# Another place and another bank for the transposed maxima of the second attention block

## The chip, the cores and the metric

The kernel runs on one core of a Trainium2 chip. The metric is the device time of one execution in microseconds. The engines that matter here: TensorE (PE in the profile; PEld is its loading of weights), VectorE (DVE), ScalarE (ACT), GpSimd (POOL), and SyncE (SP), which issues the DMAs. TensorE writes to PSUM, which has eight banks of 512 float32 values for each of 128 partitions.

## The reference

Two attention blocks with the same shapes and separate inputs, their outputs side by side. Block A attends only to the last 256 positions, block B to all.

```python
S, D, H = 2048, 512, 32          # Dh = 16
qkv = (x @ wqkv) -> q, k, v      # per head, [S, 16]
scores = q @ k.T * Dh ** -0.5    # [S, S] per head
# A only: positions outside 0 <= i - j < 256 get -1e9
p = softmax(scores, axis=-1)
out = concat_heads(p @ v) @ wo
# result: concatenate([out_A, out_B], axis=-1)
```

## The kernel before

Work is cut into *units*: one block, one group `g` of four heads (`HG`), one chunk `c` of 512 queries. Block B has 8 groups by 4 chunks, so 32 units; a unit runs over 16 key tiles of 128 keys. One key tile of one unit is a *step*.

A softmax needs each query's maximum before its exponentials. So the scores are computed twice. The first time, queries lie on the partitions: `max2` (L358) multiplies, and VectorE reduces 512 keys of each head to a maximum (L373). After the last of a unit's pieces, `max_finish` (L432) reduces what is left on VectorE (L441) and lets GpSimd negate it and split it into three bfloat16 parts (L450 to L457), in the tile `nm`. `max_rows` (L460) transposes `nm` on TensorE (L465), ScalarE copies the result from PSUM (L467, tile `ntr`), and two DMAs (L472) write it as additional rows into the query operand `oq`. The second time, keys lie on the partitions: `scores` (L488) multiplies the keys with those extended queries (L498), so that the maximum is already taken off, and ScalarE exponentiates (L505). `weigh2` (L520) multiplies the exponentials with the values (L529).

The end of the kernel's code emits block B in a fixed order, a string that is run through again and again, two steps for each pass:

```python
ORDER = "ssm4mssMs2msms2sM"
LAST = "ssss4"
```

`s` is one head's scores of the step `k`. `m` is one head's piece of maxima, `M` two heads'. A digit is that many quarters of a step's values (`weigh2`), two steps behind the scores. So a pass has 8 `s`, 8 heads' maxima (4 `m`, 2 `M`) and 8 quarters. The maxima are those of the unit after the one whose scores run, four pieces ahead of it. When none is left, `LAST` takes the place of `ORDER`.

Each kind of result has PSUM banks of its own (`view`, L194): three for the scores ("e", five in `LAST`, where the maxima's pair is added), two behind one another for `M` ("p"), one for the weighted values ("o"), and two that `room()` (L702) hands out in turn in this part of the kernel ("s"): to each `m`, to the output projection, and to the transposed maxima. A bank of "e" is taken with `M.take("e")`, which picks the one that a small time model holds free first, and given back with `release`.

A unit's last maxima are emitted at the end of a pass, where the loop's `k` is 12 of the unit's 16 steps. `max_finish` follows at once, and the unit is put on the list `rows` with a step from which it may be transposed. Ahead of the first `s` of a step the loop also emits planned work (`todo`): loads of keys, queries and values, the normalisation of finished units. The waiting unit of `rows` is looked up at the same place.

All engines run their instructions in the order of emission, each waiting for what it needs.

Of the kernel before, what the change touches and what calls it, by code (L numbers as in the profile page):

```python
# [118 lines left out]
def attention_kernel(ctx: ExitStack, tc: tile.TileContext, xT, wqk, wv, wo, out):  # L119
# [9 lines left out]
    M = Model()  # L129
# [64 lines left out]
    def view(bank):  # L194
        pool, n = bank
        first, width = {"e": (0, 1), "o": (3, 1), "p": (4, 2), "s": (6, 1)}[pool]
        n = first + width * n + (pool == "e" and n > 2)
        return ps_all[:, n] if width == 1 else ps_all[:, n:n + 2]
# [159 lines left out]
    def max2(g, c, qt, kc, heads, ps):  # L358

        m = maxima(1, g, c).rearrange("p (a r) q k -> p a r q k", a=2)  # L360
        early = g == 0 and c == 0 and heads[0] < 2
        if not early:
            follow(("k", 1, g))
            follow(("q", 1, g, c))
        for n, j in enumerate(heads):
            r, a = divmod(j, 2)
            rows = slice(ROW[a], ROW[a] + KS)
            q, k = (qe[0], ke()) if early else (opq[1, g, c][:, r], opk2(g)[:, r])
            nc.tensor.matmul(ps[:, n], q[rows, 128 * qt:128 * qt + 128], k[rows, kc * QC:kc * QC + QC], start=True,  # L369
                             stop=True)  # L370
            t = M.pe("h", 118, 0 if early else loaded(1, g, c))
        r, a = divmod(heads[0], 2)
        nc.vector.tensor_reduce(out=m[:, a:a + len(heads), r, qt, kc], in_=ps, axis=AX.X, op=ALU.max)  # L373
        return M.run("DVE", 65 + 533 * len(heads), t)
# [85 lines left out]
    def max_rows(b, g, c):  # L460
        n = f"{b}_{g}_{c}"
        nm = parts["nm"]
        bank, ps = room()
        ps = ps.bitcast(BF16)
        nc.tensor.transpose(ps[:48, :128], nm.rearrange("p a s j q -> p (a s j q)"), ident)  # L465
        nt = sb.tile([48, 128], F32, name=f"ntr_{n}", tag="ntr")
        nc.scalar.activation(nt, ps[:48, :128], AF.Copy)  # L467
        t = M.run("ACT", 200, M.pe("f", 60, ready["nm", b, g, c]))
        release(bank, t)
        for a in range(2):  # L470
            ready["q", b, g, c] = M.dma(12, t)
            nc.sync.dma_start(opq[b, g, c][ROW[a] + KS:ROW[a] + KM].bitcast(F32).rearrange(  # L472
                "s r (q t) -> s (r q) t", t=128), nt[24 * a:24 * a + 24])
# [14 lines left out]
    def scores(b, g, c, kt, j, heads=1, pieces=((),)):  # L488

        n = f"{b}_{g}_{c}_{kt}"  # L490
        pr, a0 = divmod(j, 2)
        banks = [M.take("e") for _ in range(heads)]
        ps = [view(bank) for bank in banks]
        w = QC if b else sum(x[3] for x in pieces)
        for k, col, q0, n1 in [(kt, 0, 0, QC)] if b else pieces:
            for x in range(heads):
                rows = slice(ROW[a0 + x], ROW[a0 + x] + KM)
                nc.tensor.matmul(ps[x][:, col:col + n1], opk2(g)[rows, pr, 128 * k:128 * k + 128],  # L498
                                 opq[b, g, c][rows, pr, q0:q0 + n1], start=True, stop=True)
            t = M.pe("h", 235 if b else 12 + n1 / 2.4, ready["q", b, g, c])  # L500
        if a0 == 0:
            pts[b, g, c, kt, pr] = sb.tile([128, 2, QC], F32, name=f"p_{n}_{pr}", tag="p", bufs=2 * AHEAD)
        p = pts[b, g, c, kt, pr]
        for x in range(heads):
            nc.scalar.activation(p[:, a0 + x, :w], ps[x][:, :w], AF.Exp, scale=SCALE)  # L505
            done = M.run("ACT", 60 + w / 1.2, t)
            M.release(banks[x], done)
        if b == 0:

            for d, sign, base in ((0, 1, 0), (2, -1, -1)):  # L510
                cols = [col // 128 + x for k, col, q0, n1 in pieces for x in range(n1 // 128)
                        if 4 * c + q0 // 128 + x - k == d]
                for x in cols:
                    v = p[:, :, 128 * x:128 * x + 128]
                    nc.gpsimd.affine_select(out=v, in_=v, pattern=[[0, 2], [sign, 128]], compare_op=ALU.is_ge,  # L515
                                            fill=zero_fill, base=base, channel_multiplier=-sign)
                    done = M.run("Pool", 360, done)
        ready["p", b, g, c, kt] = done
# [161 lines left out]
    def settle():  # L680

        while soon and soon[0][0] <= M.t["PE"]:
            heapq.heappop(soon)[2]()
# [9 lines left out]
    slot = [False, 0]  # L693

    def bank():
        return M.bank(pool())

    def pool():

        return min(("e",) if ns else ("e", "p"), key=lambda x: max(M.t["PE"], M.bank(x)))  # L700

    def room():  # L702

        if slot[0]:
            slot[1] ^= 1
            return None, view(("s", slot[1]))
        while bank() >= M.NEVER:
            advance()
        b = M.take(pool())
        return b, view(b)[:, 0] if b[0] == "p" else view(b)  # L710

    def release(b, t):
        if b is not None:
            M.release(b, t)

    def pop():
        now[0], _, f, a = heapq.heappop(todo)
        f(*a)
        made.add((f, *a))
# [6 lines left out]
    def advance():  # L726
        if gen[0] is None:
            while operands(proj[0][3]) >= M.NEVER:
                if soon:
                    heapq.heappop(soon)[2]()  # L730
                else:
                    pop()
            M.t["PE"] = max(M.t["PE"], operands(proj[0][3]))
            begin(heapq.heappop(proj)[3])
        try:
            next(gen[0])
        except StopIteration:
            gen[0] = None
            made.add(gen[1])
# [145 lines left out]
    while todo_a or gen[0]:  # L885
# [45 lines left out]
        if x == "t":  # L931
            un = nts.pop(0)
            max_rows(*un)
            made.add((max_rows, *un))
        elif x == "s":
            un, (m, pieces), a, z = flat[i]
# [63 lines left out]
    ns, nq, nm, half, got = 0, -8, AHEADM, 0, 0  # L1000
    t0 = M.t["PE"]
    rows = []
    while nq < 4 * len(steps):
        if nm == len(mx) and len(M.banks["e"]) == 3:
            M.banks["e"] += [M.t["PE"]] * 2
        for x in ORDER if nm < len(mx) else LAST:
            k = ns // HG
            if x == "s" and k < len(steps):
                if ns % HG == 0:
                    t = k * STEP  # L1010
                    M.t["PE"] = max(M.t["PE"], t0 + int(1000 * k * STEP))
                    settle()
                    while todo and todo[0][0] <= t:
                        pop()
                    if rows and rows[0][0] <= k:
                        max_rows(*rows.pop(0)[1])
                scores(1, *steps[k], ns % HG)
                ns += 1
            elif x in "Mm" and nm < len(mx):
                u, g, c, qt, kc = mx[nm]  # L1020
                if x == "M":
                    h = (0, 1)
                    two = view(("p", 0))
                else:
                    h = (2 + half,)
                    half ^= 1
                    two = room()[1][:, None]
                max2(g, c, qt, kc, h, two)
                got += len(h)
                if got == HG:  # L1030
                    nm += 1
                    got = 0
                    if nm % 16 == 0:
                        max_finish(1, g, c)
                        rows.append((k + 2, (1, g, c)))
            elif x.isdigit():
                if 0 <= nq < 4 * len(steps):
                    g, c, kt = steps[nq // 4]
                    q = nq % 4
                    weigh2(g, c, kt, 128 * q, 128 * (q + int(x)))  # L1040
                    if kt == NT - 1 and q + int(x) == 4:
                        unit_end(1, g, c)
                nq += int(x)
                if int(x) == 4:

                    t = k * STEP
                    two = heapq.nsmallest(2, proj)
                    if two and two[-1][0] <= t and max(operands(y[3]) for y in two) <= M.t["PE"]:
                        now[0] = t
                        for _ in two:  # L1050
                            advance()
                            while gen[0]:
                                advance()
                            t0 += 2400
# [29 lines left out]
```

## Time and profile before

| | us |
|---|---|
| median of 3 runs | 1860.56 |
| lowest, highest | 1859.86, 1864.45 |
| the profiled execution | 1862.03 |
| span of its instructions | 1860.3 |

| engine | busy us | share of the span |
|---|---|---|
| PE | 1837.5 | 99% |
| DVE | 1544.4 | 83% |
| ACT | 1408.5 | 76% |
| POOL | 469.8 | 25% |

The shares are means over the whole kernel, which has stages with different limits: block A and the projections up to about 540 us, block B's loop from there to about 1775 us, and then the last scores, values and output projections. Busy PE means that a matmul is in flight, not that the next could not have come earlier.

In the rows of the profile, `L373 DVE` is an instruction of line 373 on VectorE; `out<-in` are the program's tiles; `xN` is a count. In a group's row the figures behind the bar are the busy time in us and the mean duration in ns, then the engine's idle time just before these instructions and what ended most of it. In a row of waits: who waited, for whom, us in total, times, longest. In a row of the timeline: start and length in us, and in brackets the idle time ahead of it and what ended it; neighbours of one kind are merged into one row. In a row by stretches: the stretch and its length, then busy time (and instructions) of PE, PEld, DVE, ACT and POOL, the clock granted to TensorE (1.00 is full speed), the DMA engines' share and GB/s.

### The profile page before, as it was taken

How to read it: one execution, taken by the hardware profiler on the slowest of the kernel's cores; microseconds unless marked ns; L12 is line 12 of the kernel's file. 1: busy time of each engine (PE TensorE's matmuls, PEld its weight loads, DVE VectorE, ACT ScalarE, POOL GpSimd, SP SyncE). 2: the span in 40 equal slices, each digit the busy share in tenths (PEclk: the TensorE clock that was granted, in tenths of full speed). 3: DMA queues.
4: the chain of work that ended last, by engine and by line, in shares of the span. 5: the costliest groups of instructions: out<-in, count | busy, mean ns of one | idle time of the engine just before them, and what ended most of it. 6: DMA issues, size and time to landing. Idle time of an engine off the chain costs nothing.

```text
span 1860.3 us, 37278 instructions
## 1 busy us (share of the span) xinstructions
PE 1837.5 (99%) x14376; PEld 923.6 (50%) x14376; DVE 1544.4 (83%) x2320; ACT 1408.5 (76%) x2754; POOL 469.8 (25%) x896
## 2 busy tenths in 40 slices
PE   8999999999999999999999999999999999999999
PEld 6666656666654545444444444444444444444436
DVE  4677686766779777799999999999999999999901
ACT  4456566655558776788888888888888888889873
POOL 0367877654654331000010001000000001010010
PEclk9999999999999999999999999999999999999999
DMA  8755657544563221311300211130031130010002
GB/s 260 208 182 183 210 189 216 149 156 140 170 195 98 80 84 56 84 34 35 75 17 30 57 45 28 28 76 16 16 74 34 28 67 31 17 53 8 30 30 96
DMA packets 129153, 166.68 MB, mean 90 GB/s; under 512 B 23012, under 2 KB 58852, under 8 KB 128964
## 3 DMA queue, kind: packets, MB, share of 16 engines
q1 hardware_dynamic: 128976, 164.31, 30.4%
q8 instruction: 113, 1.85, 0.4%
q14 instruction: 64, 0.52, 0.1%
HBM read 94.49 MB, written 68.19 MB: 87 GB/s over the span
## 4 chain that ended last, share of the span: by engine, by line
PE 94%; DVE 3%; ACT 1%; POOL 1%; DMA 1%; SPq 0%; issue 0%; ACTq 0%; POOLq 0%
PE ps_all L529 29%; PE ps_all L183 19%; PE ps_all L369 19%; PE ps_all L498 19%; PE ps_all L544 4%; PE ps_all L417 3%; DVE mt L373 2%; ACT p L505 1%; PE ps_all L465 1%; DVE mt L427 1%; DMA in<-xT_A 0%; DVE ps_all L426 0%; POOL p L515 0%; POOL x L138 0%; DMA opk<-parts 0%
## 5 line engine op out<-in xcount | busy, mean ns | idle before, releaser
L505 ACT ACTIVATE p<-ps_all 128x512 f32<-128x512 f32 x2432 | 1261.6, 599 | 176.1 <-PE ps_all L498 120.0
L373 DVE TENSOR_REDUCE mt<-ps_all 128x2 f32<-128x1024 f32 x1516 | 1202.3, 868 | 83.7 <-PE ps_all L498 48.4
L498 PE MATMUL ps_all<-oq,opk 51*128 51x512 f32 (+2 forms) x2752 | 781.5, 410 | 7.7 <-ACT p L505 5.8
L369 PE MATMUL ps_all<-opk,oq 48*128 48x512 f32 x2016 | 677.6, 439 | 2.0 <-DVE mt L373 1.9
L529 PE MATMUL ps_all<-p,vt 128*32 128x256 f32 (+1 forms) x6056 | 600.1, 468 | 0.5 <-ACT ou L555 0.5
L498 PEld LDWEIGHTS ps_all<-oq,opk 51*128 51x128 f32 x2752 | 397.1, 185 | 206.6 <-ACT p L505 184.0
L369 PEld LDWEIGHTS ps_all<-opk,oq 48*128 48x128 f32 x2016 | 312.9, 185 | 321.0 <-DVE mt L373 147.9
L450 POOL TENSOR_SCALAR mm<-mm 128x16 f32<-128x16 f32 x31 | 7.9, 254 | 984.2 <-PE ps_all L498 812.8
L529 PEld LDWEIGHTS ps_all<-p,vt 128*32 128x32 f32 x6056 | 119.7, 108 | 220.7 <-issue 210.2
L515 POOL TENSOR_SCALAR_AFFINE_SELECT p<-p 128x256 f32<-128x256 f32 x480 | 180.7, 409 | 145.2 <-ACT p L505 138.6
L183 PE MATMUL ps_all<-x,w 128*128 128x512 f32 x768 | 195.3, 403 | 6.6 <-ACT x L137 6.2
L426 DVE COPY_PREDICATED ps_all<-mone,ps_all 128x256 f32<-128x256 uint16 x224 | 94.9, 424 | 91.5 <-PE ps_all L417 90.4
L183 PEld LDWEIGHTS ps_all<-x,w 128*128 128x128 f32 x768 | 140.9, 190 | 46.4 <-ACT x L137 6.4
L427 DVE TENSOR_REDUCE mt<-ps_all 128x2 f32<-128x512 f32 x224 | 155.2, 693 | 7.7
L245 ACT ACTIVATE raw<-ps_all 128x512 f32<-128x512 f32 x56 | 33.5, 598 | 103.6 <-PE ps_all L183 97.8
L544 PE MATMUL ps_all<-p,vt 128*32 128x384 f32 (+2 forms) x1408 | 97.0, 390 | 0.0
L183 PE MATMUL ps_all<-w_v,x 128*128 128x512 f32 x384 | 95.6, 398 | 0.0
L417 PE MATMUL ps_all<-opk,oq 48*128 48x384 f32 (+2 forms) x512 | 90.5, 375 | 2.2 <-DVE mt L427 1.9
L183 PE MATMUL ps_all<-w_o,x_o 128*128 128x512 f32 x384 | 90.3, 393 | 0.0
L183 PEld LDWEIGHTS ps_all<-w_o,x_o 128*128 128x128 f32 x384 | 71.2, 188 | 23.7 <-issue 8.4
L183 PEld LDWEIGHTS ps_all<-w_v,x 128*128 128x128 f32 x384 | 70.0, 188 | 18.7 <-issue 2.7
L256 POOL TENSOR_TENSOR st<-raw,st 128x512 fp32r<-128x512 f32 x56 | 72.0, 1287 | 4.7
(58 smaller groups left out, 584.5 us busy)
## 6 DMA issues: line engine op xcount, KB each, us to landing
parts<-st SPq DMA_DIRECT2D x64, 512.0 KB
oq<-parts SPq DMA_DIRECT2D x128, 128.0 KB
opk<-parts SPq DMA_DIRECT2D x128, 128.0 KB
od<-ou SPq DMA_DIRECT2D x64, 256.0 KB
vd<-vst SPq DMA_DIRECT2D x32, 272.0 KB
oq<-parts SPq DMA_DIRECT2D x128, 64.0 KB
opk<-parts SPq DMA_DIRECT2D x128, 64.0 KB
t<-od SPq DMA_DIRECT2D x32, 256.0 KB
```

What stands on the lines that cost most here:

```text
L183: nc.tensor.matmul(ps, l(u), r(v), start=start and k == 0, stop=stop and k == n - 1)
L256: nc.gpsimd.tensor_sub(two[:, 1], raw, two[:, 0].bitcast(F32))
L369: nc.tensor.matmul(ps[:, n], q[rows, 128 * qt:128 * qt + 128], k[rows, kc * QC:kc * QC + QC], start=True, stop=True)
L373: nc.vector.tensor_reduce(out=m[:, a:a + len(heads), r, qt, kc], in_=ps, axis=AX.X, op=ALU.max)
L417: nc.tensor.matmul(two[:, a, 0:w], opq[b, g, c][rows, r, 128 * qt:128 * qt + 128], opk2(g)[rows, r, t0:t1], start=True, stop=True)
L426: nc.vector.copy_predicated(two[:, :, 256:384], later, two[:, :, 0:128])
L427: nc.vector.tensor_reduce(out=m[:, :, r, qt, 0], in_=two[:, :, 128:384], axis=AX.X, op=ALU.max)
L498: nc.tensor.matmul(ps[x][:, col:col + n1], opk2(g)[rows, pr, 128 * k:128 * k + 128], opq[b, g, c][rows, pr, q0:q0 + n1], start=True, stop= ...
L505: nc.scalar.activation(p[:, a0 + x, :w], ps[x][:, :w], AF.Exp, scale=SCALE)
L515: nc.gpsimd.affine_select(out=v, in_=v, pattern=[[0, 2], [sign, 128]], compare_op=ALU.is_ge, fill=zero_fill, base=base, channel_multiplier ...
L529: nc.tensor.matmul(o[32 * j:32 * j + 32, q0:q1], vt[(g // 2) % 2][:, kt, vc:vc + 32], pts[1, g, c, kt, j // 2][:, j % 2, q0:q1], start=kt ...
L544: nc.tensor.matmul(o[32 * j:32 * j + 32, q0:q0 + w], vt[(g // 2) % 2][:, kt, vc:vc + 32], pts[b, g, c, m, j // 2][:, j % 2, col:col + w], ...
```

## The change

Three things change, all for block B's loop alone (`slot[0]` is true only there). The transposed maxima take a bank of the scores' ("e") instead of one from `room()`. The unit is put on the list with step `k + 1` instead of `k + 2`. And the list is looked up behind the last values of a pass, where `nq`, the count of quarters, is a multiple of 8, and no longer ahead of a step's first `s`. In a pass of `ORDER`, the transposition so stands behind the last `2` and ahead of the `s` and `M` that end the pass of steps 12 and 13; before, it stood behind that `M`, ahead of the first `s` of step 14. In `LAST` it stands behind the `4`.

```diff
@@ def max_rows(b, g, c)
         nm = parts["nm"]
-        bank, ps = room()
+        if slot[0]:
+
+            bank = M.take("e")
+            ps = view(bank)
+        else:
+            bank, ps = room()
         ps = ps.bitcast(BF16)
         nc.tensor.transpose(ps[:48, :128], nm.rearrange("p a s j q -> p (a s j q)"), ident)
@@ the loop, ahead of a step's first s
                     while todo and todo[0][0] <= t:
                         pop()
-                    if rows and rows[0][0] <= k:
-                        max_rows(*rows.pop(0)[1])
                 scores(1, *steps[k], ns % HG)
@@ the loop, M and m
                         max_finish(1, g, c)
-                        rows.append((k + 2, (1, g, c)))
+                        rows.append((k + 1, (1, g, c)))
@@ the loop, a digit
                 nq += int(x)
+
+                if rows and rows[0][0] <= k and nq % 8 == 0:
+                    max_rows(*rows.pop(0)[1])
                 if int(x) == 4:
```

## The prediction

> **What bounds the kernel now.** I read the page's head and its chain of waits first, then the table by stretches for the steady part of the second block (920 to 1760 us), then the groups of lines and the waits in that stretch, and last the timeline around one transposition, one instruction at a time.
>
> ```profile
> span 1860.3 us, 37278 instructions
> PE 94%; DVE 3%; ACT 1%; POOL 1%; DMA 1%; SPq 0%; issue 0%; ACTq 0%; POOLq 0%
> 920.00:1760.00 840.00, 839.43 (x7067) 347.53 (x7066) 830.55 (x1090) 745.50 (x1457) 60.45 (x144) 1.00 0.14 37
> ```
>
> The chain names PE for 94%, but PE's matmuls are pipelined and overlap, so a PE that always has one in flight is not yet a PE at its limit. In the steady stretch VectorE (third busy figure) works 830.55 of 840.00 us. ScalarE has 94 us to spare, GpSimd nearly everything. The 9.45 us that VectorE idles are named one by one:
>
> ```profile
> L373 DVE TENSOR_REDUCE mt<-ps_all 128x1 f32<-128x512 f32 (+1 forms) x1057 | 825.9, 858 | 7.2 <-PE ps_all L498 6.1 <-PE ps_all L369 1.0
> L441 DVE TENSOR_REDUCE mm<-mt 128x16 f32<-128x64 f32 x22 | 4.8, 220 | 2.3
> PEld ps_all L369 <- DVE mt L373: 108.1, 233, 0.8
> PEld ps_all L498 <- ACT p L505: 100.4, 333, 0.8
> DVE mt L373 <- PE ps_all L498: 6.1, 22, 0.3
> ```
>
> L441 runs 22 times here, once for each unit (one group of four heads by 512 queries), so a unit takes 840 / 22 = 38.18 us. Its 2.3 us of idle time stay, since L441 reads what the last L373 wrote. The other wait, 22 times 0.28 us, is also once for each unit. PE itself waits 108.1 us for VectorE's banks and 100.4 us for ScalarE's: everywhere else VectorE is the one that is waited for. So **VectorE bounds this stretch**, and only what makes VectorE idle can be saved there.
>
> The timeline of TensorE shows where the once-a-unit wait lies: first a disturbed end and start of ORDER's pass, then, in the second fence, the next and undisturbed ones.
>
> ```profile
> 1159.92 0.64 PE L529 MATMUL ps_all<-p,vt 128*32 128x256 f32 x8
> 1160.49 0.49 PE L498 MATMUL ps_all<-oq,opk 51*128 51x512 f32 x1
> 1160.63 0.58 PE L369 MATMUL ps_all<-opk,oq 48*128 48x512 f32 x2
> 1161.23 0.22 PE L465 MATMUL ps_all<-ident,nm 128*48 128x128 bf16 x1
> 1161.37 0.50 PE L498 MATMUL ps_all<-oq,opk 51*128 51x512 f32 x2
> 1161.83 0.49 PE L369 MATMUL ps_all<-opk,oq 48*128 48x512 f32 x1
> 1162.25 1.06 PE L529 MATMUL ps_all<-p,vt 128*32 128x512 f32 x8
> 1163.24 0.49 PE L369 MATMUL ps_all<-opk,oq 48*128 48x512 f32 x1
> ```
>
> ```profile
> 1166.00 0.49 PE L498 MATMUL ps_all<-oq,opk 51*128 51x512 f32 x1
> 1166.01 0.72 PE L369 MATMUL ps_all<-opk,oq 48*128 48x512 f32 x2
> 1166.35 0.62 PE L498 MATMUL ps_all<-oq,opk 51*128 51x512 f32 x2
> 1166.59 0.40 PE L369 MATMUL ps_all<-opk,oq 48*128 48x512 f32 x1
> 1166.91 1.06 PE L529 MATMUL ps_all<-p,vt 128*32 128x512 f32 x8
> ```
>
> Read each as: last score and pair of maxima (s, M), then s s m of the next pass, then the four weighted values, then the second m. Undisturbed, the weighted values start 0.91 us after the last score (1166.00 to 1166.91); with the transposition 1.76 us (1160.49 to 1162.25). VectorE's instructions, each from its own narrow window:
>
> ```profile
> 1160.49 0.68 DVE L373 TENSOR_REDUCE mt<-ps_all 128x1 f32<-128x512 f32 x1
> 1161.09 0.68 DVE L373 TENSOR_REDUCE mt<-ps_all 128x1 f32<-128x512 f32 x1
> 1161.69 1.22 DVE L373 TENSOR_REDUCE mt<-ps_all 128x2 f32<-128x1024 f32 x1
> 1162.82 0.68 DVE L373 TENSOR_REDUCE mt<-ps_all 128x1 f32<-128x512 f32 x1
> 1163.77 0.69 DVE L373 TENSOR_REDUCE mt<-ps_all 128x1 f32<-128x512 f32 x1 [0.27 <-PE ps_all L498]
> 1166.11 0.68 DVE L373 TENSOR_REDUCE mt<-ps_all 128x1 f32<-128x512 f32 x1
> 1166.77 1.23 DVE L373 TENSOR_REDUCE mt<-ps_all 128x2 f32<-128x1024 f32 x1
> ```
>
> The transposition takes a bank of the maxima's own two. It waits until VectorE has left it (1160.49 + 0.68 = 1161.17; it starts at 1161.23), and the alternation is shifted by one, so that the next m has to wait for the *later* of the two (1161.09 + 0.68 = 1161.77; it starts at 1161.83). PE's queue is in order: the weighted values stand behind that m, the second m behind them, and it ends at 1163.24 + 0.49 = 1163.73. VectorE had been ready for it at 1162.82 + 0.60 = 1163.42 (singles follow one another every 0.60 us, 1160.49 to 1161.09).
>
> **The change part by part.**
>
> *The loss that goes.* At that second m VectorE loses 1163.77 - 1163.42 = 0.35 us: the gap of 0.27 and the 0.08 by which reductions otherwise overlap. The same lateness costs 1166.77 - 1166.11 - 0.60 = 0.06 us at the next pass's last pair. With the stretch's mean gap (6.1 / 22 = 0.28) that is 0.28 + 0.08 + 0.06 = 0.42 us a unit. How many units:
>
> ```profile
> DVE mt L373 <- PE ps_all L498: 1.1, 4, 0.3
> DVE mt L373 <- PE ps_all L498: 0.3, 1, 0.3
> DVE mt L373 <- PE ps_all L498: 0.4, 1, 0.4
> ```
>
> 22 in the steady stretch, 4 from 770 to 920 us, one from 582 to 588 us, one from 681 to 686 us, and one more with the second row's figures from 730 to 735 us: 29 of the loop's 31. One of the other two stands among projections, one in the last stretch, where no maxima are left; both count nothing. **29 x 0.42 = 12.2 us.**
>
> *The transposition behind the values.* It does not leave PE; it goes ahead of s and M. In the rows it starts when the matmuls ahead have ended (1160.63 + 0.58 = 1161.21, then 1161.23), and the next score follows 0.14 later. Behind the values that end at 1159.92 + 0.64 = 1160.56 it would start at 1160.57, and the score at 1160.71 instead of 1160.49: 0.22 us late. Bounds: 0.14, if it overlaps the values' tail as that score does now, and 0.49, a whole score's duration, if it held the array as long as one; nothing makes the score earlier, since it only gains something ahead of it. I take 0.22, measured on this very instruction. M then ends 0.73 us after the score's start (1166.00 to 1166.01 + 0.72) at 1161.44. VectorE wants M at 1161.69, so 0.25 us cover a delay that may thus grow to 0.47. Cost: nothing; without the cover, each 0.1 us would be 3 us.
>
> *The bank of the scores.* Three banks go round. With one turn taken by the transposition, each of the next three scores needs an exponential later by one:
>
> ```profile
> 1160.27 0.59 ACT L505 ACTIVATE p<-ps_all 128x512 f32<-128x512 f32 x1
> 1161.52 0.26 ACT L467 ACTIVATE ntr<-ps_all 48x128 f32<-48x128 bf16 x1
> 1166.48 0.18 PEld L498 LDWEIGHTS ps_all<-oq,opk 51*128 51x128 f32 x1 [0.18 <-ACT p L505]
> ```
>
> From the undisturbed rows, the pass's scores come 0.35 us (1166.35) and, by the load at 1166.48 and an estimated 0.09 to its matmul (1166.59, the m loaded beside it, has 0.11), 0.57 us after the last score, so at 1161.06 and 1161.28. The first needs the exponential that ends at 1160.86. The second needs the copy out of the transposition: transposition's end 1160.57 + 0.22 = 1160.79, copy 0.07 later as now (1161.45 to 1161.52), 0.26 long, end 1161.12; with the same 0.07 to the score's load and 0.09 from there to its matmul that is 1161.28. It just fits. The m no longer waits: its bank is free at 1161.17, it comes at 1161.30 (0.59 after the score). Values at 1161.62, the second m at 1162.61 (0.99 behind, as 1162.25 to 1163.24), its end 0.49 later at 1163.10, and VectorE wants it at 1163.42: 0.32 us in hand where 0.31 were missing. If the copy came later than that, it would cost only what exceeds 0.32.
>
> The Trainium skill says in "Perfetto Trace Analysis", section "Optimizing Tensor Performance", that independent matmul groups should rotate through different PSUM banks so that emptying one overlaps the next group's matmuls. For the scores this speaks against the change, since it takes one of their three turns, and for the maxima it speaks for it; the 333 waits of scores for exponentials agree that the former has a price. It is the slower rival below.
>
> *Inputs of the transposition.* It moves 1161.23 - 1160.57 = 0.66 us forward, towards GpSimd's last step:
>
> ```profile
> 1159.51 0.22 POOL L457 TENSOR_TENSOR nm<-nr,nm 128x16 bf16<-128x16 f32 x1
> 1161.80 1.57 SPq L472 DMA_DIRECT2D oq<-ntr  x2
> ```
>
> Ready at 1159.73, 0.84 us early. The two row DMAs move with it, past nothing: SyncE issues nothing else from 1159 to 1166 us. Whoever needs the rows, the next unit's scores at 1166.35, gets them earlier. The last transposition, where no maxima are left, keeps its place in PE's order and takes one of five banks there: nothing, at most its own 0.3 us either way.
>
> **The sum.** 12.2 us from the profiled execution's 1862.03 (span 1860.3 and 1.7 around it) gives 1849.8. The median shown, 1860.56, lies 1.47 below that execution: **1848.4 us**.
>
> **The rivals.**
>
> *The clock's drop goes or stays (rival on the fast side).* Behind the last maxima PE pauses for VectorE, and the granted clock halves:
>
> ```profile
> 1768.90:1775.80 6.90, 6.81 (x26) 2.02 (x28) 0.26 (x2) 3.91 (x8) 4.21 (x8) 0.51 0.00 0
> 1773.15 1.93 PE L529 MATMUL ps_all<-p,vt 128*32 128x512 f32 x8
> 1776.14 1.06 PE L529 MATMUL ps_all<-p,vt 128*32 128x512 f32 x8
> 1778.07 1.06 PE L529 MATMUL ps_all<-p,vt 128*32 128x512 f32 x8
> ```
>
> A step then takes 2.99 us (1773.15 to 1776.14, with the last transposition in it) instead of 1.93, so 6.9 us hold 2.3 steps and cost 2.3 x 1.06 = 2.4 us. Everything ahead of it shifts by 12 us; if the drop fails to come, the time is 1848.4 - 2.4 = 1846.0. Against it: the pause itself is the change of order at the end of the maxima, which stays. The Trainium skill, "TensorE: Matmul & The Clock Gate", section "What's actually happening", has the gate judge activity in a window that runs free of the kernel, so the same pause could pass; one trace cannot show that.
>
> *Half stays.* The copy is late by 0.5 us (one more exponential ahead of it), and the second m misses VectorE by about 0.2: 6 us remain, 1854.5. Against it: the copy stands directly behind the exponential of 1160.27.
>
> *Nothing is gained.* The wait only moves: M comes as late as the second m does now. 1860.6. It needs a delay of 0.47 + 0.42 us where 0.22 was worked out.
>
> *Slower: the scores' ring becomes the bound.* If the turn taken costs the ring of scores and exponentials a whole exponential and the copy (0.50 + 0.26) beyond the 0.22, M is late by 0.98 - 0.47 = 0.51 us, and the next pass's pair again, some 0.2: 0.71 - 0.42 = 0.29 us lost net, 29 times, 8.4 us, 1869.0. It decides from 0.89 us of delay. For it: PE already waits 100.4 us for exponentials. Against: the exponentials needed end 0.2 us ahead of their scores.
>
> **How the numbers follow.** Whole loss gone, clock as before: 0.61 (its own range 1847 to 1850). The same without the drop: 0.12. Half: 0.12. Nothing: 0.07. Slower: 0.08. The range 1845.2 to 1855 holds the first three. About 0.3% (5.6 us) is what a measurement of this kernel can tell from no change; faster by more than that: the first two and most of the third, 0.84; within it 0.08; slower 0.08.
>
> **What would show it.** Right: L373's idle time behind L498 in the steady stretch goes from 6.1 us to below 1, the second m starts 1.9 us behind the last score instead of 2.75, a unit takes about 37.76 us, and PE's waits for VectorE grow. Wrong: a gap ahead of the two-bank L373 (M late), a score waiting for L467, or L465 waiting for GpSimd.

## The result and the profile after

| | before | after |
|---|---|---|
| median of 6 runs, us | 1861.05 | 1849.89 |
| lowest, highest | 1859.26, 1864.45 | 1844.76, 1851.65 |
| profiled execution, its span | 1862.03, 1860.3 | 1845.59, 1843.9 |

The ratio after to before is 0.9931 (95% interval 0.992 to 0.9943), 11 to 15 us. The range given holds the median; 1848.4 was forecast.

The table by stretches, the groups of VectorE and the waits, all from 920 to 1760 us of the changed kernel (its code has five more lines behind L463, so L498 is L503 here, L465 is L470, L529 is L534):

```profile
920.00:1760.00 840.00, 838.04 (x7131) 351.64 (x7123) 832.25 (x1096) 756.02 (x1474) 64.33 (x152) 1.00 0.15 37
```

```profile
L373 DVE TENSOR_REDUCE mt<-ps_all 128x1 f32<-128x512 f32 (+1 forms) x1063 | 827.4, 856 | 0.9 <-PE ps_all L369 0.8
L441 DVE TENSOR_REDUCE mm<-mt 128x16 f32<-128x64 f32 x23 | 5.1, 220 | 2.4
```

```profile
PEld ps_all L369 <- DVE mt L373: 158.4, 278, 0.8
PEld ps_all L503 <- ACT p L510: 92.7, 314, 0.8
```

The wait of L373 behind a score, 6.1 us in 22 pieces, is gone; the row has 0.9 us left, 0.8 of them behind maxima, and VectorE's other idle time is the 2.4 us ahead of L441, which must read the last reduction. (This stretch reaches 5 us past the last maxima, which is why VectorE's busy total is not higher still.) TensorE now waits for VectorE 158.4 us instead of 108.1: an engine that is not late waits more for the one that bounds. Around one transposition, the timeline of TensorE and VectorE's instructions, each from a narrow window:

```profile
1153.39 0.64 PE L534 MATMUL ps_all<-p,vt 128*32 128x256 f32 x8
1153.96 0.24 PE L470 MATMUL ps_all<-ident,nm 128*48 128x128 bf16 x1
1154.13 0.50 PE L503 MATMUL ps_all<-oq,opk 51*128 51x512 f32 x1
1154.13 0.73 PE L369 MATMUL ps_all<-opk,oq 48*128 48x512 f32 x2
1154.47 0.62 PE L503 MATMUL ps_all<-oq,opk 51*128 51x512 f32 x2
1154.73 0.46 PE L369 MATMUL ps_all<-opk,oq 48*128 48x512 f32 x1
1155.12 1.06 PE L534 MATMUL ps_all<-p,vt 128*32 128x512 f32 x8
1156.11 0.50 PE L369 MATMUL ps_all<-opk,oq 48*128 48x512 f32 x1
```

```profile
1155.15 1.21 DVE L373 TENSOR_REDUCE mt<-ps_all 128x2 f32<-128x1024 f32 x1
1156.28 0.68 DVE L373 TENSOR_REDUCE mt<-ps_all 128x1 f32<-128x512 f32 x1
```

The weighted values start 0.99 us behind the last score (1154.13 to 1155.12), where it was 1.76. M ends at 1154.86 and is wanted at 1155.15; the second m ends at 1156.61 and is wanted 0.60 behind 1156.28, at 1156.88. Both are in time, by 0.29 and 0.27 us.

A good ruler for the loop is L441, which runs once for each of the 32 units. These are its rows in the view of its source line, before and after, with the first and the last start:

```profile
L441 DVE TENSOR_REDUCE mm<-mt x32: 219/220/222, 534.0 to 1769.0; 128x16 f32<-128x64 f32 x32
```

```profile
L441 DVE TENSOR_REDUCE mm<-mt x32: 219/220/221, 533.8 to 1755.3; 128x16 f32<-128x64 f32 x32
```

The loop takes 1221.5 us instead of 1235.0: **13.5 us**. What follows its last L441 up to the span's end takes 88.6 instead of 91.3: 2.7 us less. There the granted clock differs: behind the last maxima the changed kernel's profiled execution kept full speed where the other fell to half.

```profile
1756.00:1763.00 7.00, 7.00 (x48) 2.19 (x48) 0.00 (x0) 6.92 (x16) 3.91 (x7) 1.00 0.01 4
```

The mean granted clock differs from run to run, in both kernels. With 0.998 the changed kernel took 1844.76 and 1845.59, with 0.994 to 0.996 it took 1849.36 to 1851.65. Where the clock fell is known of the profiled executions alone.

### The profile page after: what moved, and what is told of

It reads as the page before. It is cut to its first block, busy times and chain, and to the rows that moved or that the text cites. A ratio compares the mean times of both kernels' runs of the same rounds, so it can differ in the third digit from the quotient of the medians.

```text
span 1843.9 us, 37250 instructions
## 1 busy us (share of the span) xinstructions
PE 1821.1 (99%) x14376; PEld 924.7 (50%) x14376; DVE 1539.2 (83%) x2320; ACT 1410.2 (76%) x2754; POOL 469.7 (25%) x896
## 4 chain that ended last, share of the span: by engine, by line
PE 91%; DVE 6%; ACT 1%; DMA 1%; POOL 0%; SPq 0%; issue 0%; ACTq 0%; DVEq 0%
PE ps_all L534 28%; PE ps_all L183 19%; PE ps_all L369 19%; PE ps_all L503 18%; DVE mt L373 5%; PE ps_all L549 4%; PE ps_all L417 3%; ACT p L510 1%; DVE mt L427 1%; PE ps_all L470 1%; DMA in<-xT_A 0%; DVE ps_all L426 0%; POOL p L520 0%; DMA opk<-parts 0%; POOL x L138 0%
## 5 line engine op out<-in xcount | busy, mean ns | idle before, releaser
L373 DVE TENSOR_REDUCE mt<-ps_all 128x2 f32<-128x1024 f32 x1516 | 1197.5, 865 | 74.9 <-PE ps_all L369 40.1
L503 PE MATMUL ps_all<-oq,opk 51*128 51x512 f32 (+2 forms) x2752 | 783.6, 407 | 7.6 <-ACT p L510 5.7
L534 PE MATMUL ps_all<-p,vt 128*32 128x256 f32 (+1 forms) x6056 | 598.3, 467 | 0.5 <-ACT ou L560 0.5
L503 PEld LDWEIGHTS ps_all<-oq,opk 51*128 51x128 f32 x2752 | 400.5, 185 | 191.6 <-ACT p L510 170.4
L369 PEld LDWEIGHTS ps_all<-opk,oq 48*128 48x128 f32 x2016 | 306.8, 185 | 311.7 <-DVE mt L373 209.7
L534 PEld LDWEIGHTS ps_all<-p,vt 128*32 128x32 f32 x6056 | 119.5, 108 | 225.8 <-issue 215.3
L646 ACT ACTIVATE ob<-ps_all 128x512 f32<-128x512 f32 x32 | 19.2, 599 | 71.3 <-PE ps_all L183 45.9
```

Source lines behind the costliest of these rows:

```text
L534: nc.tensor.matmul(o[32 * j:32 * j + 32, q0:q1], vt[(g // 2) % 2][:, kt, vc:vc + 32], pts[1, g, c, kt, j // 2][:, j % 2, q0:q1], start=kt ...
```

## The experiments

All loops below are from the first to the last L441 of the profiled execution, all tails from there to the span's end.

### The two halves of the change

Is it the bank, the place, or both? First the bank alone:

```diff
-        bank, ps = room()
+        if slot[0]:
+            bank = M.take("e")
+            ps = view(bank)
+        else:
+            bank, ps = room()
```

> Only the bank changes: the transposition stays ahead of the first score of step 14, with step k + 2, but takes one of the scores' three banks. My theory: the loss before had two halves, the transposition's wait (for a maxima's bank, and behind M) and the shifted alternation of the maxima's two banks. Here the alternation is whole again, but the second of the next two scores now needs the exponential of the last score ahead of the transposition (it ends at 1161.62 in the trace of before, so that score comes at about 1161.77 and the m behind it with it, values at about 1162.1 instead of 1162.25). VectorE's loss falls from 0.42 us a unit to about 0.2: 5 to 7 us faster than before, about 1855. Rival, the alternation alone was the cause: all of the 11 us, 1850. Rival, the place alone was: nothing, 1861.

1856.03 us against 1862.32 (ratio 0.9972, interval 0.9959 to 0.9985); loop 1230.0. The timeline of TensorE at one transposition (L469 here, scores L502, values L533):

```profile
1158.58 0.50 PE L502 MATMUL ps_all<-oq,opk 51*128 51x512 f32 x1
1158.71 0.60 PE L369 MATMUL ps_all<-opk,oq 48*128 48x512 f32 x2
1159.24 0.24 PE L469 MATMUL ps_all<-ident,nm 128*48 128x128 bf16 x1
1159.41 0.85 PE L502 MATMUL ps_all<-oq,opk 51*128 51x512 f32 x2
1159.76 0.50 PE L369 MATMUL ps_all<-opk,oq 48*128 48x512 f32 x1
1160.19 1.06 PE L533 MATMUL ps_all<-p,vt 128*32 128x512 f32 x8
```

The values start 1.61 us behind the last score, as worked out, between 0.99 and 1.76. The m is no longer held by a bank; the pair of scores is, 0.85 us long where 0.62 is usual, since its second one needs the exponential of the score ahead of the transposition. The loop is 5.1 us shorter, 0.16 us a unit: the rival "alternation alone" falls, and so does the one by which the bank alone gives nothing. Most of what is left comes from the place: undisturbed, the first score of the pair starts 0.35 us behind the last score of the pass ahead, and here 0.83, since the transposition stands behind M. That is 0.48 of the 0.70 us by which the values are later than the undisturbed 0.91; the other 0.22 are lost from the pair on.

Then the place alone, the changed kernel without the bank:

```diff
-        if slot[0]:
-            bank = M.take("e")
-            ps = view(bank)
-        else:
-            bank, ps = room()
+        bank, ps = room()
```

> Only the place changes: the transposition stands behind the last values of steps 12 and 13, but takes a maxima's bank as before. My theory: it then waits for that bank ahead of s and M (VectorE leaves the bank at 1161.17 in the trace of before), so M ends at about 1162.10 where VectorE wants it at 1161.69: a gap of about 0.4 us ahead of the two-bank L373 in place of the one ahead of the one-bank L373, the same loss as before within 0.1 us a unit: 1858 to 1864. Rival, the place alone was the cause: all of the 11 us, 1850.

1860.65 us (ratio 0.9995, interval 0.9986 to 1.0004); loop 1234.9, as before the change. Rows of TensorE's timeline, and of VectorE's groups by shape from 920 to 1760 us:

```profile
1162.06 0.64 PE L529 MATMUL ps_all<-p,vt 128*32 128x256 f32 x8
1163.36 0.22 PE L465 MATMUL ps_all<-ident,nm 128*48 128x128 bf16 x1 [0.66 <-DVE mt L373]
```

```profile
L373 DVE TENSOR_REDUCE mt<-ps_all 128x1 f32<-128x512 f32 x705 | 452.5, 687 | 0.1
L373 DVE TENSOR_REDUCE mt<-ps_all 128x2 f32<-128x1024 f32 x352 | 430.7, 1224 | 8.9 <-PE ps_all L498 7.6 <-PE ps_all L369 1.4
```

TensorE stands 0.66 us idle until VectorE leaves the maxima's bank, M is late, and the gap has moved from the one-bank reduction to the two-bank one: the wait changed its place and kept its price. So the halves are worth 5.1 and 0.1 us, and together 13.5. The place alone puts the wait for the maxima's bank ahead of M, and the bank alone leaves the transposition behind M. Only with both does it start early and without a wait.

### What the cover is worth

Three more transpositions behind the first, in the changed kernel:

```diff
+        for _ in range(3 if slot[0] else 0):
+            nc.tensor.transpose(ps[:48, :128], nm.rearrange("p a s j q -> p (a s j q)"), ident)
         nt = sb.tile([48, 128], F32, name=f"ntr_{n}", tag="ntr")
```

> The changed kernel with three more transpositions of the same maxima to the same bank right behind the first, in block B's loop: nothing is computed that is used, and only TensorE gets more work at that place. My theory, that TensorE has some 0.27 to 0.29 us in hand there (M ends at 1154.86 where VectorE wants it at 1155.15, the second m at 1156.61 where VectorE wants it at 1156.88, both in the trace after): each transposition costs about 0.17 us (distance from it to the next score), so three cost 0.5 us and VectorE loses about 0.2 us a unit: gaps ahead of L373, 5 to 8 us slower than the changed kernel. Rival, TensorE has far more in hand: no difference, no gaps. Rival, TensorE was the bound all along: 0.5 us a unit, 15 us slower.

1845.43 us, loop 1221.8 instead of 1221.5: no difference. But this did not show that there is far more in hand, for the price in the expectation was wrong:

```profile
1154.28 0.24 PE L470 MATMUL ps_all<-ident,nm 128*48 128x128 bf16 x1
1154.36 0.33 PE L472 MATMUL ps_all<-ident,nm 128*48 128x128 bf16 x3
1154.62 0.50 PE L505 MATMUL ps_all<-oq,opk 51*128 51x512 f32 x1
1154.62 0.73 PE L369 MATMUL ps_all<-opk,oq 48*128 48x512 f32 x2
```

```profile
1155.47 1.22 DVE L373 TENSOR_REDUCE mt<-ps_all 128x2 f32<-128x1024 f32 x1
```

The next score is 0.34 us behind the first transposition instead of 0.17: three cost 0.17 us, not 0.5. M ends at 1155.35 and is wanted at 1155.47, so 0.12 of the 0.29 us are left, which is what three at that price should leave. With sixteen, the cover must break (the same edit with 16):

> As the run with three more transpositions, with sixteen more. There, three delayed the next score by 0.17 us (0.34 us behind the first transposition instead of 0.17), 0.057 each and not 0.17, and left M 0.12 of its 0.29 us. My theory: the cover of 0.29 us is real and only the price of a transposition was wrong; sixteen delay the score by 0.91 us, so VectorE gets gaps of about 0.6 us ahead of the two-bank L373, once a unit, and the loop is 29 x 0.6 = 16 to 20 us longer than the changed kernel's 1221.5 (first L441 to last). Rival, TensorE has no such limit here: loop within 2 us of the changed kernel's. Rival, TensorE bounds: 31 x 0.91 = 28 us.

1869.96 us, loop 1241.6, 20.1 longer than the changed kernel's and just above the 16 to 20 expected. TensorE's timeline and VectorE's:

```profile
1164.13 0.24 PE L470 MATMUL ps_all<-ident,nm 128*48 128x128 bf16 x1
1164.20 1.06 PE L472 MATMUL ps_all<-ident,nm 128*48 128x128 bf16 x16
1165.19 0.50 PE L505 MATMUL ps_all<-oq,opk 51*128 51x512 f32 x1
```

```profile
1161.79 3.60 DVE L373 TENSOR_REDUCE mt<-ps_all 128x1 f32<-128x512 f32 x5
1165.96 22.17 DVE L373 TENSOR_REDUCE mt<-ps_all 128x2 f32<-128x1024 f32 x28 [0.56 <-PE ps_all L505]
```

The score is 1.06 us behind, 0.89 more than with one. Less the 0.29 in hand that is 0.60, and the gap ahead of the two-bank reduction is 0.56 and the overlap that it breaks 0.08. The 20.1 us are 0.65 for each of 31 units. The cover is real, and its size is right. (The time grew by 24 us against the changed kernel on the same chip; 3.6 of the rest lie behind the loop, where this execution's clock fell as before the change.)

From the other side, no transposition at all (the row DMAs take the transposed maxima of block B's first unit each time, so the exponentials of the others are taken off a maximum that is not theirs):

```diff
+            nt = parts["nt"]
+            for a in range(2):
+                nc.sync.dma_start(opq[b, g, c][ROW[a] + KS:ROW[a] + KM].bitcast(F32).rearrange(
+                    "s r (q t) -> s (r q) t", t=128), nt[24 * a:24 * a + 24])
+            ready["q", b, g, c] = M.dma(12, M.dma(12, ready["nm", b, g, c]))
+            return
+        if slot[0]:
...
         nc.scalar.activation(nt, ps[:48, :128], AF.Copy)
+        parts["nt"] = nt
```

> The changed kernel without transposition and copy in block B's loop; the row DMAs take the transposed maxima of block B's first unit each time, so the second block's exponentials are taken off another unit's maxima. My theory: the transposition is wholly hidden after the change, VectorE has no gap but the one ahead of L441 and so nothing is to be gained: a unit takes the same 37.55 or 37.75 us within 0.03, the loop's length is that of the changed kernel within 1 us. Rival, part of its cost is still there: up to 0.17 us a unit less, 5 us.

1848.41 us, loop 1221.3, 0.2 us less than with it; the mean distance of L441, over 24 units, is 37.70 us without and 37.71 with it. The transposition costs nothing any more. (The four runs have mean clocks of 0.995 to 0.997, so their times say less here than the loop.)

### The clock behind the last maxima

The changed kernel again, beside the others:

> The changed kernel again, unaltered, beside the others on one chip. Theory, that its runs differ by whether and how long the granted clock drops behind the last maxima: runs with a mean clock of 0.998 at 1844.5 to 1846, with 0.996 or less at 1848 to 1852, none between by more than 1 us from these. Rival, the spread has nothing to do with the clock: times and mean clocks without order.

1845.88 us as the median of four: 0.998 with 1844.30, 1844.98 and 1846.79, 0.994 with 1850.90. The order by clock is there, though 1846.79 lies 0.8 above the band given and 1844.30 lies 0.2 below it. The execution of 1846.79 is the profiled one: its loop is 1221.6 us and its tail 88.6, as in the changed kernel's first profile, but its first L441 starts at 534.9 us instead of 533.8, so most of its difference lies ahead of the loop.

Apart from the two with an edit at the banks further below, the tail of the profiled executions is 88.5 to 88.7 us without a fall of the clock behind the last maxima, 89.7 and 89.8 with one of 3.4 us (in the runs without transposition and with the place alone), and 91.3 with one of 6.8 us (before). In the run with sixteen more it is 92.2, with a fall of 6.8 us in which the last unit's sixteen stand too. So the fall in the profile before was worth 2.7 us.

All eleven profiled executions have one more fall, of 6.8 us, at the start of the loop, between 549.8 and 560.3 us; a mean clock of 0.998 contains it. The execution with the place alone has yet another at 263 us, in block A. So a mean clock of 0.994 to 0.996 tells that there were further falls, but not that they lay behind the last maxima.

Does TensorE's pause at that point cause it?

```diff
         if nm == len(mx) and len(M.banks["e"]) == 3:
-            M.banks["e"] += [M.t["PE"]] * 2
+            M.banks["e"] += [M.t["PE"] + 2500] * 2
```

> The changed kernel with one line changed where LAST takes over: the maxima's two banks join the scores' 2.5 us later in the time model, so that the scores behind the last maxima first go round the three banks that ScalarE frees and do not wait for VectorE's last reduction; the order of instructions is the same. Theory, TensorE's pause of 1.4 to 1.9 us there lets the clock drop: without it no run drops there, all of them have a mean clock of 0.997 or more, and take 1843 to 1846. Rival, the drop comes from what lies ahead (or at random): as many runs with 0.994 to 0.996 as of the changed kernel (4 of 6 there).

1845.56 us: clocks 0.998, 0.998, 0.998 and 0.997, times 1845.46 to 1845.60 and 1847.86, the last of them above the range given. TensorE's rows behind the last maxima, before the change, of the changed kernel and of this one:

```profile
1767.15 0.39 PE L498 MATMUL ps_all<-oq,opk 51*128 51x512 f32 x1
1768.99 1.22 PE L498 MATMUL ps_all<-oq,opk 51*128 51x512 f32 x3 [1.44 <-DVE mt L373]
```

```profile
1753.08 0.73 PE L369 MATMUL ps_all<-opk,oq 48*128 48x512 f32 x2
1753.41 0.40 PE L503 MATMUL ps_all<-oq,opk 51*128 51x512 f32 x1
1755.26 0.73 PE L503 MATMUL ps_all<-oq,opk 51*128 51x512 f32 x3 [1.45 <-DVE mt L373]
```

```profile
1754.00 0.63 PE L503 MATMUL ps_all<-oq,opk 51*128 51x512 f32 x2
1754.84 0.99 PE L503 MATMUL ps_all<-oq,opk 51*128 51x512 f32 x2 [0.21 <-ACT p L510]
```

The pause of 1.45 us is 0.21, the tail 87.8 instead of 88.6. But three of four runs at 0.998 say little beside three of four of the changed kernel on the same chip, and the last run below, without the pause as well, has one execution with 0.996. That the pause causes the fall is not shown.

The kept traces show that it does not decide alone. Nine of them have this pause, 1.43 to 1.46 us long. Four have a fall at its end or up to 0.8 us behind it (before, the place alone, sixteen more, no transposition), and five have none (the changed kernel twice, the bank alone, three more, and the next run below). What separates the four from the five is the pause's place in a grid of time. In the clock records the falls last 3.41 or 6.83 us, and full speed between two falls lasts, for instance, 286.72, 1198.08, 1211.73 or 1218.56 us: whole multiples of 3.413. Counted in such steps from the fall at the start of the loop, the pause lies within one step in the four (before: it lasts from 1767.55 to 1768.99, the step from 1765.53 to 1768.94, so all but 0.05 us). In the five a step ends inside it and leaves at most 1.3 us on one side (changed kernel: from 1753.81 to 1755.26, a step ends at 1754.73). This is a pattern in nine traces and not an experiment, since no run moves the pause against the steps on purpose. It also does not cover every fall: the step ahead of the one at 263 us holds only 0.4 us without a matmul.

### What bounds the loop now

If VectorE does, then its one idle spot that is left is worth its length.

```diff
-    rows = []
+    rows, ends = [], []
...
+                if ends:
+                    max_finish(*ends.pop())
                 got += len(h)
...
-                        max_finish(1, g, c)
+                        if nm < len(mx):
+                            ends.append((1, g, c))
+                        else:
+                            max_finish(1, g, c)
                         rows.append((k + 1, (1, g, c)))
```

> The changed kernel with max_finish one maximum later: L441 stands behind the next unit's first m instead of straight behind the reduction that it reads. Theory, VectorE bounds the loop with no gap left but the one ahead of L441 (0.10 us idle and 0.08 of overlap): that 0.19 us a unit goes, and as M and the second m have 0.29 and 0.27 us in hand after the change, TensorE keeps up: L441's distance falls from 37.71 to about 37.53 us, the loop from 1221.5 to about 1216, the time by 5 to 6 us at the same clock. Rival, the bound has passed to TensorE or ScalarE with the change: same times within 1 us. Rival, GpSimd's parts now come too late for the transposition (0.77 us in hand, 0.4 to 0.6 taken): L470 waits, gaps ahead of L373, slower.

1841.68 us (ratio to before 0.9895, interval 0.988 to 0.991); loop 1216.7, 4.8 us less than the changed kernel's, a little under the 5 to 6 expected; L441 every 37.51 us instead of 37.71. VectorE's groups:

```profile
L373 DVE TENSOR_REDUCE mt<-ps_all 128x1 f32<-128x512 f32 (+1 forms) x1064 | 827.7, 848 | 0.9 <-PE ps_all L369 0.6 <-PE ps_all L503 0.2
L441 DVE TENSOR_REDUCE mm<-mt 128x16 f32<-128x64 f32 x23 | 4.6, 199 | 0.1
```

The 2.4 us ahead of L441 are 0.1 and nothing took their place: VectorE bounds the loop, and neither rival holds: the time did change, and L373 got no new gaps. With the edit at the banks as well:

> The two last edits together: max_finish one maximum later, and the maxima's banks joining the scores' later. If they add up: the loop of the former (1216.7), the tail of the latter (87.8), 1839.9 with a clock of 0.998, and few or no runs with less than 0.997. Rival, the shorter loop has the pause and the drop back: a tail of 88.5 to 91, 1841 to 1845.

1841.40 us, median of five (0.9898, interval 0.988 to 0.9916); loop 1216.1, tail 87.8, and the times 1838.34 and 1841.26 at a clock of 0.998, 1841.40 and 1842.19 at 0.997, 1844.61 at 0.996. Loop and tail add up in the profiled execution, so the rival of a longer tail falls. Its time, 1841.26, is nevertheless 1.4 us above the 1839.9 given, because its first L441 starts at 535.6 us and not at 533.8; in the medians the second edit can't be told from the clock. This version and the one ahead of it are the fastest here, about 3 to 6 us below the changed kernel at a clock of 0.998.

## Why the prediction was right

**The place of the loss** was right: a VectorE that bounds, made idle once a unit by the second m. The place where the loss goes was right too: the gap is gone, the second m starts 1.98 us behind the last score (1154.13 to 1156.11) where 1.9 was forecast and 2.75 stood before, the unit is 37.71 us long where 37.76 was forecast, and the two halves of the change behave as its two waits say.

**The size** was somewhat low: 29 x 0.42 = 12.2 us against 13.5 in the loop. A unit became 0.45 us shorter by L441's distance (38.16 to 37.71), 0.03 more than the two places in the timeline had shown. And all 31 distances between one L441 and the next are shorter, not 29: 30 of them by 0.35 to 0.58 us and the first, among the projections, by 0.15. What the 0.03 consist of was not looked for.

**The transposition's delay** was put at 0.22 us and is 0.17: the score comes 0.74 us after the values' start (1153.39 to 1154.13) instead of 0.57. It starts ahead of the values' shown end (1153.96, the end at 1154.03), as a score did before, so the lower bound of 0.14 was nearer than the value taken. The cover of M, 0.25 by the forecast, is 0.29; that of the second m, 0.32, is 0.27; GpSimd's, 0.84, is 0.77. All hold.

**The slower rival's point of decision**, a delay of 0.89 us, was tried by the sixteen more: a delay of 1.06 us made the loop 6.6 us longer than before the change (1241.6 against 1235.0), and (1.06 - 0.89) x 31 is 5.3. So the delay from which the change would lose was about right, and the change is far on the good side of it. That run delays by transpositions; that the scores' ring could cause such a delay is not shown. The ring does pay for the turn taken where the transposition stands ahead of the pair (the bank alone): 0.85 us for a pair that otherwise takes 0.62. In the changed kernel, with the turn taken as well, the pair takes 0.62. The Trainium skill, "Perfetto Trace Analysis", section "Optimizing Tensor Performance", has independent matmul groups rotate through different PSUM banks; the pair of 0.85 us agrees with that, and the pair of 0.62 shows that one turn less costs nothing here where what frees the bank is early.

**The clock** was taken as a drop that the profile of before has and that stays or goes with the change, and it was held to stay because TensorE's pause stays, though the same pause, it said, could pass. That is the weak step of the forecast. The pause did stay, 1.45 us after and 1.44 before, and the drop was not there in the profiled execution, which took 1845.59 where the rival on the fast side gave 1846.0. In both kernels the mean clock varies between the runs. The 2.4 us worked out for the drop were 2.7.

Compared like with like, the change is worth 14 to 15 us, the loop's 13.5 among them: of the runs of before beside the first four experiments, 5 of 17 had 0.998, at 1858.50 to 1859.56 us, and of those beside the changed kernel's second measurement two, at 1859.72 and 1860.68; the changed kernel's five runs with 0.998 took 1844.30 to 1846.79. The medians of the first comparison gave 11.2, as four of the six runs after had 0.994 to 0.996. So it is in part luck that the median, 1849.89, lies only 1.5 us from the forecast: the loop gave 1.3 us more than the sum, and the lower clock in most of those runs took more than that back.

## What to carry to other kernels

An odd user of a pair of alternating buffers can cost twice, as it did here: it waits for its own turn, and it shifts everybody behind it onto the buffer that comes free later. When such a user has to be placed, look for the ring and the place together: the buffer must have been free for long where it stands, and what stands right behind it must have time in hand. Where the idle time of the bounding engine is named piece by piece, its pieces tell what such an edit can give.

## What was not expected of the hardware

A second transposition of the same kind costs TensorE far less than the first: 0.17 us to the next score for one, 0.34 for four, 1.06 for seventeen, so 0.056 to 0.057 us each behind the first. And the granted clock falls to half for 3.4 or 6.8 us, in all eleven traces at the start of the loop, and behind the last maxima in four of nine traces with the same pause of TensorE. There it went with the pause lying within one step of 3.413 us of the clock's records, and in the three traces without added work in that stretch it was worth 1.1 to 2.7 us.
